# ReLU²-attention and SwiGLU feed-forward on one core: Q and K transposed by DMA, feed-forward in column halves, weights staged as float32

## The chip, the cores and the metric

The kernel runs on one core of a Trainium2 chip. The metric is the device time of one execution in microseconds (us), lower is better. The kernel before takes 549.85 us (median of 2 runs, 547.66 to 552.03). On three chips, the same kernel took 547.41, 548.23 and 549.57 us (median of 7 runs each), so differences of 1% between calls mean little; kernels of one call share a chip.

## The reference

```python
# attention: q, k, v are (8 batches, 12 heads, 448 rows, 64)
scores = scale * q @ k.T
attn   = maximum(scores, 0) ** 2 / S
x      = attn @ v              # reordered to (3584 tokens, 768)
# feed-forward: w_gate, w_val (768, 1536), w_out (1536, 768), all float32
xn  = x / sqrt(mean(x*x) + 1e-6) * rms_g
out = (silu(xn @ w_gate) * (xn @ w_val)) @ w_out
```

## The kernel before

The kernel works in bfloat16 and interleaves two streams on the engines: the feed-forward of batch b is the main stream, and attention of batch b+1, with its norm, is spread between the main stream's units. Program order fixes the order on each engine; only semaphores join the engines. PE is the matmul engine, DVE, ACT and Pool are the vector, scalar and general engines, SP issues DMAs, and SBUF is the memory on the chip. These are the parts that matter here (cuts marked with `...`).

```python
ldpool = tile_pool(name="ld", bufs=2)                 # q, k, v of a batch, two of each
...
def load_w(which, s):                                 # weights: a DMA from Pool's queue casts to bf16
    nc.gpsimd.dma_start(out=dst[:, :, s*FS:(s+1)*FS], in_=...)
...
def reorder(b, j):                                    # on DVE, for each pair of heads
    for nm in ("q", "k"):
        nc.vector.tensor_copy(out=t..., in_=ld[nm, b][:, 2*j:2*j+2, :]...)
def transposes(b, j):                                 # on PE, 8 of them, then copied by DVE
    ...
    nc.tensor.transpose(out=psT[...], in_=ldp[nm, b, j][:, c, :, :], identity=ident[:])
    nc.vector.tensor_copy(out=t[:], in_=psT[:])
def scores(b, j, cs):  ...                            # K x Q, ReLU (3 of 4 on ACT), square on DVE
def attend(b, j):      ...                            # A*V: 8 matmuls, each 64 columns of the array wide
def project(w_sb, b, fb, nm):                         # feed-forward: 6 matmuls, 128 columns wide
    for kt in range(KT):
        nc.tensor.matmul(out=ps[:], lhsT=w_sb[:, kt, fb*P:(fb+1)*P], rhs=xns[b][:, kt, :], ...)
...
for b in range(B):
    side = attention(b + 1) + [(1.1, lambda b=b: norm(b + 1))]
    alloc_ld(b + 2)
    for nm in ("q", "k", "v"):
        load(nm, b + 2)                               # Pool's queue, casting DMA
    for fn in merge(ffn(b), side, 0.0, 0.1):          # side units end 10% before the main stream
        fn()
```

Of the kernel before, what the change touches and what calls it, by code (L numbers as in the profile page):

```python
# [9 lines left out]
I32 = mybir.dt.int32  # L10
# [4 lines left out]
NCH = 4  # L15
# [3 lines left out]

# [17 lines left out]
def kernel(  # L37
# [22 lines left out]
    NT = 2 * S // P  # L60

# [4 lines left out]
    ldpool = ctx.enter_context(tc.tile_pool(name="ld", bufs=2))  # L66
    tpool = ctx.enter_context(tc.tile_pool(name="tsb", bufs=2))
    apool = ctx.enter_context(tc.tile_pool(name="attn", bufs=10))
    xpool = ctx.enter_context(tc.tile_pool(name="xT", bufs=2))
    npool = ctx.enter_context(tc.tile_pool(name="norm", bufs=2))  # L70
    hpool = ctx.enter_context(tc.tile_pool(name="hT", bufs=2))
# [4 lines left out]
    ps_m = ctx.enter_context(tc.tile_pool(name="ps_m", bufs=3, space=bass.MemoryType.PSUM))  # L76

# [6 lines left out]
    def alloc_ld(b):  # L84
        for nm in ("q", "k", "v"):
            ld[nm, b] = ldpool.tile([PC, H, NCH * D], BF16, name=nm + "b", tag=nm + "b")

    def load(nm, b, h0=0, h1=H):
        src = {"q": q, "k": k, "v": v}[nm]
        nc.gpsimd.dma_start(out=ld[nm, b][:, h0:h1, :], in_=head_rows(src, b, h0, h1))  # L90
# [4 lines left out]
    NSL = 4  # L95
    FS = F // NSL

    def load_w(which, s):
        dst, src = {"g": (wg_sb, moe_w_gate), "v": (wv_sb, moe_w_val)}[which]
        nc.gpsimd.dma_start(  # L100
            out=dst[:, :, s * FS : (s + 1) * FS],
            in_=src.rearrange("(kt p) f -> p kt f", p=P)[:, :, s * FS : (s + 1) * FS],
        )

    def load_wo(s, n):
        w = FT // n
        nc.gpsimd.dma_start(
            out=wo_sb[:, s * w : (s + 1) * w, :],
            in_=moe_w_out.rearrange("(fk p) m -> p fk m", p=P)[:, s * w : (s + 1) * w, :],
        )  # L110

    alloc_ld(0)
    load("q", 0, 0, 2)
    load("k", 0, 0, 2)
    ident = const.tile([PC, PC], BF16, name="ident", tag="ident")
    masks.make_identity(nc, ident[:])
    ones_bf = const.tile([P, P], BF16, name="ones_bf", tag="ones_bf")
    nc.vector.memset(ones_bf[:], 1.0)
    eps_col = const.tile([P, 1], FP32, name="eps_col", tag="eps_col")
    nc.vector.memset(eps_col[:], eps)  # L120
    g_sb = wpool.tile([P, KT], FP32, name="g_sb", tag="rmsg")
    nc.sync.dma_start(out=g_sb[:], in_=moe_rms_g.rearrange("(kt p) -> p kt", p=P))
    load("q", 0, 2, 6)
    load("k", 0, 2, 6)
    load("v", 0, 0, 6)
    load("q", 0, 6, 12)
    load("k", 0, 6, 12)
    load("v", 0, 6, 12)
    for s in range(NSL):
        load_w("g", s)  # L130
        load_w("v", s)
        if s == 1:
            alloc_ld(1)
            load("q", 1)
            load("k", 1)
    load("v", 1)
    load_wo(0, 2)
    load_wo(1, 2)


    xTs = {}
    qkT = {}
    ldp = {}

    def reorder(b, j):
        for nm in ("q", "k"):
            t = tpool.tile([PC, NCH, 2, D], BF16, name=nm + "p", tag=nm + "p")
            nc.vector.tensor_copy(  # L148
                out=t[:].rearrange("p c h d -> p h c d"),
                in_=ld[nm, b][:, 2 * j : 2 * j + 2, :].rearrange("p h (c d) -> p h c d", c=NCH),  # L150
            )
            ldp[nm, b, j] = t

    def transposes(b, j):
        if j == 0:
            xTs[b] = xpool.tile([P, KT, S], BF16, name="xT", tag="xT")
            reorder(b, 0)
        if j + 1 < HP:
            reorder(b, j + 1)
        psT = ps_a.tile([P, 2, S], BF16, name="psT", tag="ps_a")  # L160
        for ti, nm in enumerate(("q", "k")):
            for c in range(NCH):
                nc.tensor.transpose(  # L163
                    out=psT[:, ti, c * PC : (c + 1) * PC],
                    in_=ldp[nm, b, j][:, c, :, :],
                    identity=ident[:],
                )
        t = tpool.tile([P, 2, S], BF16, name="qkT", tag="qkT")
        nc.vector.tensor_copy(out=t[:], in_=psT[:])  # L169
        qkT[b, j] = t  # L170

    rsq = {}
    state = {"n": 0}

    def scores(b, j, cs):
        t = qkT[b, j]
        pss = []
        for c in cs:
            psS = ps_s.tile([PC, 2, 512], FP32, name="psS", tag="psS")
            for hh in range(2):  # L180
                prt = slice(hh * D, (hh + 1) * D)
                nc.tensor.matmul(  # L182
                    out=psS[:, hh, :S],
                    lhsT=t[prt, 1, c * PC : (c + 1) * PC],
                    rhs=t[prt, 0, :],
                    start=True,
                    stop=True,
                )
            pss.append(psS)
        for c, psS in zip(cs, pss):  # L190
            r = apool.tile([PC, 2, S], BF16, name="r", tag="r")
            on_dve = state["n"] % 4 == 3
            state["n"] += 1
            if on_dve:
                nc.vector.tensor_relu(out=r[:], in_=psS[:, :, :S])  # L195
            else:
                nc.scalar.activation(out=r[:], in_=psS[:, :, :S], func=ACT.Relu)  # L197
            nc.vector.tensor_tensor(out=r[:], in0=r[:], in1=r[:], op=ALU.mult)  # L198
            rsq[b, j, c] = r

    x2s = {}

    def attend(b, j):
        psAV = ps_a.tile([P, S], FP32, name="psAV", tag="ps_a")
        for c in range(NCH):
            for hh in range(2):
# [6 lines left out]
                )  # L213
        xT = xTs[b]
        nc.scalar.mul(out=xT[:, j, :], in_=psAV[:], mul=inv_attn)  # L215
        if j == 0:
# [141 lines left out]
```

## Time and profile before

| | before |
|---|---|
| time, us | 549.85 |
| span of the profiled run, us | 544.9 |
| PE / DVE / ACT busy | 89% / 62% / 46% |
| reciprocal of the norm, batch 0, 1, 7, at us | 43.95, 108.41, 491.14 |
| so one batch takes (491.14 - 108.41) / 6, us | 63.8 |

One reciprocal on DVE belongs to the norm of each batch, so the times between reciprocals give the period of a batch.

From the page of the kernel before: the span, the busy time of PE (share of the span, x instructions), and the chain of waits that ended last, by engine.

```profile
span 544.9 us, 7394 instructions
PE 485.1 (89%) x3024; PEld 236.1 (43%) x3024; DVE 338.6 (62%) x586; ACT 252.3 (46%) x369; POOL 34.4 (6%) x45
...
PE 73%; DVE 14%; ACT 8%; issue 2%; DMA 1%; POOL 0%; ACTq 0%; POOLq 0%
```

PE is the bound, and the chain runs over PE for 73% of the span.

The timeline of PE around the boundary between two batches (start us, length us, engine, line, operation, output and inputs, count; in brackets the idle time before it and who ended it):

```profile
236.43 1.48 PE L238 MATMUL psSS<-x_1924,ones_bf 128*128 128x448 bf16 x6
237.75 5.37 PE L286 MATMUL psO<-wo_sb,hT 128*128 128x256 bf16 x36
245.97 0.37 PE L163 MATMUL psT<-ident,qp 112*128 112x112 bf16 x4 [2.85 <-DVE qp L148]
246.18 0.36 PE L163 MATMUL psT<-ident,kp 112*128 112x112 bf16 x4
246.38 1.30 PE L260 MATMUL psG<-xn,wg_sb 128*128 128x448 bf16 x6
247.52 1.30 PE L260 MATMUL psV<-xn,wv_sb 128*128 128x448 bf16 x6
```

The output projection of one batch ends, PE idles 2.85 us for the reordered Q (which stands on DVE behind the norm), then come the transposes and the first gate. A group of six feed-forward matmuls starts every 1.14 us (246.38 to 247.52).

### The profile page before, as it was taken

How to read it: one execution, taken by the hardware profiler on the slowest of the kernel's cores; microseconds unless marked ns; L12 is line 12 of the kernel's file. 1: busy time of each engine (PE TensorE's matmuls, PEld its weight loads, DVE VectorE, ACT ScalarE, POOL GpSimd, SP SyncE). 2: the span in 40 equal slices, each digit the busy share in tenths (PEclk: the TensorE clock that was granted, in tenths of full speed). 3: DMA queues.
4: the chain of work that ended last, by engine and by line, in shares of the span. 5: the costliest groups of instructions: out<-in, count | busy, mean ns of one | idle time of the engine just before them, and what ended most of it. 6: DMA issues, size and time to landing. Idle time of an engine off the chain costs nothing.

```text
span 544.9 us, 7394 instructions
## 1 busy us (share of the span) xinstructions
PE 485.1 (89%) x3024; PEld 236.1 (43%) x3024; DVE 338.6 (62%) x586; ACT 252.3 (46%) x369; POOL 34.4 (6%) x45
## 2 busy tenths in 40 slices
PE   3774999879999799888999799987999899989996
PEld 1331444434444344444444444444445444444553
DVE  3886677467764677566774677656775677745210
ACT  2553454524545354535444454454545445553221
POOL 7330001000010001000010000100000000000000
PEclk9976999979999899999999999999999999999999
DMA  9999938150073402560054500733001200002013
GB/s 114 201 201 205 203 53 102 35 103 1 1 102 73 95 1 24 79 123 16 1 75 86 108 1 1 103 58 80 1 1 29 78 10 2 1 29 59 0 30 88
DMA packets 45858, 35.08 MB, mean 64 GB/s; under 512 B 2304, under 2 KB 42240, under 8 KB 45824
## 3 DMA queue, kind: packets, MB, share of 16 engines
q0 software_dynamic: 40560, 23.60, 31.7%
q1 hardware_dynamic: 5264, 11.02, 6.8%
q8 instruction: 23, 0.38, 0.3%
q14 instruction: 11, 0.09, 0.1%
HBM read 47.19 MB, written 11.01 MB: 107 GB/s over the span
## 4 chain that ended last, share of the span: by engine, by line
PE 73%; DVE 14%; ACT 8%; issue 2%; DMA 1%; POOL 0%; ACTq 0%; POOLq 0%
PE psV L260 20%; PE psG L260 20%; PE psO L286 14%; PE psAV L207 8%; PE psS L182 8%; DVE xn L249 5%; DVE rstd L246 4%; ACT r L197 4%; PE psT L163 3%; ACT L243 2%; DVE r L198 2%; DVE r L195 1%; ACT rstd L243 1%; DMA kb<-in_k_dram 1%; ACT xT L215 1%
## 5 line engine op out<-in xcount | busy, mean ns | idle before, releaser
L198 DVE TENSOR_TENSOR r<-r 112x896 bf16<-112x896 bf16 x192 | 119.3, 625 | 93.8 <-ACT r L197 91.9
L197 ACT ACTIVATE r<-psS 112x896 bf16<-112x896 f32 x144 | 127.0, 916 | 52.5 <-PE psS L182 52.4
L260 PE MATMUL psG<-xn,wg_sb 128*128 128x448 bf16 x576 | 129.4, 360 | 1.1 <-DVE xn L249 1.0
L260 PE MATMUL psV<-xn,wv_sb 128*128 128x448 bf16 x576 | 128.0, 359 | 0.0
L286 PE MATMUL psO<-wo_sb,hT 128*128 128x512 bf16 (+1 forms) x672 | 115.2, 326 | 0.0
L271 ACT ACTIVATE sil<-psG 128x448 bf16<-128x448 f32 x96 | 52.3, 545 | 102.2 <-PE psG L260 90.8
L277 DVE TENSOR_TENSOR hT<-sil,psV 128x448 bf16<-128x448 bf16 x96 | 59.4, 618 | 45.9 <-PE psV L260 37.8
L286 PEld LDWEIGHTS <-hT 128*128 128x128 bf16 x672 | 63.6, 98 | 49.2 <-issue 9.3
L182 PE MATMUL psS<-qkT 64*112 64x448 bf16 x384 | 64.5, 394 | 19.3 <-ACT r L197 7.4
L260 PEld LDWEIGHTS <-wg_sb 128*128 128x128 bf16 x576 | 53.0, 99 | 59.8 <-issue 19.2
L260 PEld LDWEIGHTS <-wv_sb 128*128 128x128 bf16 x576 | 52.3, 99 | 57.5 <-issue 19.2
L293 ACT COPY ost<-psO 128x512 f32<-128x512 f32 (+1 forms) x56 | 26.9, 480 | 81.4 <-PE psO L286 81.4
L195 DVE TENSOR_SCALAR r<-psS 112x896 bf16<-112x896 f32 x48 | 52.0, 1084 | 0.0
L207 PE MATMUL psAV<-r,vb 112*64 112x448 bf16 x384 | 47.7, 370 | 4.6 <-DVE qkT L169 3.8
L182 PEld LDWEIGHTS <-qkT 64*112 64x112 bf16 x384 | 21.1, 131 | 60.5 <-issue 55.2
L163 PE MATMUL psT<-ident,qp 112*128 112x112 bf16 x192 | 19.0, 226 | 29.6 <-DVE qp L148 29.6
L215 ACT ACTIVATE xT<-psAV 128x448 bf16<-128x448 f32 x48 | 26.1, 545 | 33.7 <-PE psAV L207 33.7
L163 PEld LDWEIGHTS <-qp 112*128 112x128 bf16 x192 | 14.0, 103 | 40.9 <-DVE qp L148 31.9
L207 PEld LDWEIGHTS <-vb 112*64 112x64 bf16 x384 | 19.1, 111 | 28.9 <-issue 21.4
L246 DVE RECIPROCAL rstd<-rstd 128x448 f32<-128x448 f32 x8 | 23.6, 2953 | 12.8 <-ACT rstd L243 12.8
L169 DVE COPY qkT<-psT 128x896 bf16<-128x896 bf16 x48 | 29.8, 620 | 2.3 <-PE psT L163 2.1
L249 DVE SCALAR_TENSOR_TENSOR xn<-xT,g_sb,rstd 128x448 bf16<-128x448 bf16 x48 | 29.3, 680 | 0.3
(39 smaller groups left out, 157.6 us busy)
## 6 DMA issues: line engine op xcount, KB each, us to landing
qb<-in_q_dram POOLq DMA_DIRECT2D x7, 672.0 KB, 7.3
kb<-in_k_dram POOLq DMA_DIRECT2D x7, 672.0 KB, 9.8
vb<-in_v_dram POOLq DMA_DIRECT2D x7, 672.0 KB, 8.1
out_dram<-ost SPq DMA_DIRECT2D x8, 336.0 KB, 2.8
wg_sb<-in_moe_w_gate_dram POOLq DMA_DIRECT2D x4, 576.0 KB, 20.2
wv_sb<-in_moe_w_val_dram POOLq DMA_DIRECT2D x4, 576.0 KB, 21.8
wo_sb<-in_moe_w_out_dram POOLq DMA_DIRECT2D x2, 1152.0 KB, 28.3
out_dram<-ost SPq DMA_DIRECT2D x8, 288.0 KB, 5.3
```

The costliest lines, as they stand in the source:

```text
L163: nc.tensor.transpose(out=psT[:, ti, c * PC : (c + 1) * PC], in_=ldp[nm, b, j][:, c, :, :], identity=ident[:],)
L182: nc.tensor.matmul(out=psS[:, hh, :S], lhsT=t[prt, 1, c * PC : (c + 1) * PC], rhs=t[prt, 0, :], start=True, stop=True,)
L195: nc.vector.tensor_relu(out=r[:], in_=psS[:, :, :S])
L197: nc.scalar.activation(out=r[:], in_=psS[:, :, :S], func=ACT.Relu)
L198: nc.vector.tensor_tensor(out=r[:], in0=r[:], in1=r[:], op=ALU.mult)
L207: nc.tensor.matmul(out=psAV[hh * D : (hh + 1) * D, :], lhsT=ld["v", b][:, 2 * j + hh, c * D : (c + 1) * D], rhs=rsq[b, j, c][:, hh, :], st ...
L246: nc.vector.reciprocal(out=rstd[:], in_=rstd[:])
L249: nc.vector.scalar_tensor_tensor(out=xn[:, kt, :], in0=xTs[b][:, kt, :], scalar=g_sb[:, kt : kt + 1], in1=rstd[:], op0=ALU.mult, op1=ALU.mult,
L260: nc.tensor.matmul(out=ps[:], lhsT=w_sb[:, kt, fb * P : (fb + 1) * P], rhs=xns[b][:, kt, :], start=(kt == 0), stop=(kt == KT - 1),)
L271: nc.scalar.activation(out=s[:], in_=psG[:], func=ACT.Silu)
L277: nc.vector.tensor_tensor(out=hTs[b // 2][:, fb, o : o + S], in0=sil[b, fb][:], in1=psV[:], op=ALU.mult)
L286: nc.tensor.matmul(out=ps[:, :w], lhsT=hTs[i][:, fk, t * P : (t + 1) * P], rhs=wo_sb[:, fk, o : o + w], start=(fk == 0), stop=(fk == FT - 1),)
```

## The change

It has four parts.

1. Q and K of batches 2 to 7 are reordered by two large DVE copies and transposed by two DMA transposes issued by SP. Batches 0 and 1 keep transposes on PE, now without reorder.
2. All feed-forward matmuls, and the sum of squares, are issued as two halves of 64 columns, the tiling that A*V already had.
3. The weights come as float32 by SP's DMA queue into a pool of 7 staging buffers, and Pool casts them.
4. To make room, `q` and `k` have one buffer instead of two, and so have the pools of the attention output and of the norm. DVE takes one ReLU in six instead of one in four. Attention of batch 1 is spread over the last 70% of the first feed-forward, to its very end.

```diff
-    ldpool = ctx.enter_context(tc.tile_pool(name="ld", bufs=2))
+    ldpool = ctx.enter_context(tc.tile_pool(name="ld", bufs=1))          # v keeps bufs=2
 ...
+    def fetch_w(which, s):                       # SP, float32 into the staging pool
+        ...
+        return nc.sync.dma_start(out=st[:], in_=src)
+    def cast_w(which, s, eng):                   # eng is nc.gpsimd
+        eng.tensor_copy(out=dst, in_=st[:])
 ...
+    def reorder(b):
+        t = late["reord"].tile([PC, 2, NCH, H, D], BF16, name="kqp", tag="kqp")
+        for ti, nm in enumerate(("k", "q")):
+            nc.vector.tensor_copy(out=t[:, ti]..., in_=ld[nm, b][:]...)
+    def dma_transposes(b):
+        t = tpool.tile([P, 2, NCH, HP, PC], BF16, name="kqT", tag="kqT", bufs=1)
+        for ti in range(2):
+            nc.sync.dma_start_transpose(out=t[:, ti]..., in_=src[:, ti]...)
 ...
+    def halves(ps, w, lhsT, rhs, start, stop):
+        for hf in range(2):
+            prt = slice(hf * HALF, (hf + 1) * HALF)
+            nc.tensor.matmul(out=ps[prt, :w], lhsT=lhsT[:, prt], rhs=rhs, start=start, stop=stop)
 ...
-            side = attention(b + 1) + [(1.1, lambda b=b: norm(b + 1))]
+            side = attention(b + 1, False)
+            def prepare(b=b):
+                if b + 2 < B:
+                    reorder(b + 2)
+                    dma_transposes(b + 2)
+            side += [(0.0, prepare), (1.1, lambda b=b: norm(b + 1))]
         if b + 2 < B:
             alloc_ld(b + 2)
             for nm in ("q", "k", "v"):
                 load(nm, b + 2)
```

More of the change, by code (lines that the diff above doesn't have):

```diff
@@ L9 @@
 FP32 = mybir.dt.float32
-I32 = mybir.dt.int32
 BF16 = mybir.dt.bfloat16
@@ L60 @@
     NT = 2 * S // P
+    HALF = P // 2
     ctx.enter_context(tc.manual_schedule())
@@ L65 @@
     wpool = ctx.enter_context(tc.tile_pool(name="weights", bufs=1))
-    ldpool = ctx.enter_context(tc.tile_pool(name="ld", bufs=2))
+    ldpool = ctx.enter_context(tc.tile_pool(name="ld", bufs=1))
     tpool = ctx.enter_context(tc.tile_pool(name="tsb", bufs=2))
     apool = ctx.enter_context(tc.tile_pool(name="attn", bufs=10))
-    xpool = ctx.enter_context(tc.tile_pool(name="xT", bufs=2))
-    npool = ctx.enter_context(tc.tile_pool(name="norm", bufs=2))
-    hpool = ctx.enter_context(tc.tile_pool(name="hT", bufs=2))
+    xpool = ctx.enter_context(tc.tile_pool(name="xT", bufs=1))
+    npool = ctx.enter_context(tc.tile_pool(name="norm", bufs=1))
+    hpool = ctx.enter_context(tc.tile_pool(name="hT", bufs=1))
     spool = ctx.enter_context(tc.tile_pool(name="sig", bufs=3))
@@ L76 @@
     ps_m = ctx.enter_context(tc.tile_pool(name="ps_m", bufs=3, space=bass.MemoryType.PSUM))
+    late = {}
     def head_rows(t, b, h0, h1):
@@ L84, in alloc_ld @@
     def alloc_ld(b):
-        for nm in ("q", "k", "v"):
+        for nm in ("q", "k"):
             ld[nm, b] = ldpool.tile([PC, H, NCH * D], BF16, name=nm + "b", tag=nm + "b")
+        ld["v", b] = ldpool.tile([PC, H, NCH * D], BF16, name="vb", tag="vb", bufs=2)
     def load(nm, b, h0=0, h1=H):
         src = {"q": q, "k": k, "v": v}[nm]
-        nc.gpsimd.dma_start(out=ld[nm, b][:, h0:h1, :], in_=head_rows(src, b, h0, h1))
+        return nc.gpsimd.dma_start(out=ld[nm, b][:, h0:h1, :], in_=head_rows(src, b, h0, h1))
     wg_sb = wpool.tile([P, KT, F], BF16, name="wg_sb", tag="wg")
@@ L94 @@
     wo_sb = wpool.tile([P, FT, DM], BF16, name="wo_sb", tag="wo")
-    NSL = 4
+    NSL = 6
     FS = F // NSL
-    def load_w(which, s):
-        dst, src = {"g": (wg_sb, moe_w_gate), "v": (wv_sb, moe_w_val)}[which]
-        nc.gpsimd.dma_start(
-            out=dst[:, :, s * FS : (s + 1) * FS],
-            in_=src.rearrange("(kt p) f -> p kt f", p=P)[:, :, s * FS : (s + 1) * FS],
-        )
-    def load_wo(s, n):
-        w = FT // n
-        nc.gpsimd.dma_start(
-            out=wo_sb[:, s * w : (s + 1) * w, :],
-            in_=moe_w_out.rearrange("(fk p) m -> p fk m", p=P)[:, s * w : (s + 1) * w, :],
-        )
@@ L112 @@
-    alloc_ld(0)
-    load("q", 0, 0, 2)
-    load("k", 0, 0, 2)
-    ident = const.tile([PC, PC], BF16, name="ident", tag="ident")
-    masks.make_identity(nc, ident[:])
-    ones_bf = const.tile([P, P], BF16, name="ones_bf", tag="ones_bf")
-    nc.vector.memset(ones_bf[:], 1.0)
-    eps_col = const.tile([P, 1], FP32, name="eps_col", tag="eps_col")
-    nc.vector.memset(eps_col[:], eps)
-    g_sb = wpool.tile([P, KT], FP32, name="g_sb", tag="rmsg")
-    nc.sync.dma_start(out=g_sb[:], in_=moe_rms_g.rearrange("(kt p) -> p kt", p=P))
@@ L123 @@
-    load("q", 0, 2, 6)
-    load("k", 0, 2, 6)
-    load("v", 0, 0, 6)
-    load("q", 0, 6, 12)
-    load("k", 0, 6, 12)
-    load("v", 0, 6, 12)
-    for s in range(NSL):
-        load_w("g", s)
-        load_w("v", s)
-        if s == 1:
-            alloc_ld(1)
-            load("q", 1)
-            load("k", 1)
-    load("v", 1)
-    load_wo(0, 2)
-    load_wo(1, 2)
+    stage = {}
+    def fetch_w(which, s):
+        if which == "o":
+            st = late["stage"].tile([P, 2, DM], FP32, name="wst", tag="wst")
+            src = moe_w_out.rearrange("(fk p) m -> p fk m", p=P)[:, 2 * s : 2 * s + 2, :]
+        else:
+            st = late["stage"].tile([P, KT, FS], FP32, name="wst", tag="wst")
+            w = {"g": moe_w_gate, "v": moe_w_val}[which]
+            src = w.rearrange("(kt p) f -> p kt f", p=P)[:, :, s * FS : (s + 1) * FS]
+        stage[which, s] = st
+        return nc.sync.dma_start(out=st[:], in_=src)
@@ L141 @@
+    def cast_w(which, s, eng):
+        st = stage.pop((which, s))
+        if which == "o":
+            dst = wo_sb[:, 2 * s : 2 * s + 2, :]
+        else:
+            dst = {"g": wg_sb, "v": wv_sb}[which][:, :, s * FS : (s + 1) * FS]
+        if eng is nc.scalar:
+            eng.copy(out=dst, in_=st[:])
+        else:
+            eng.tensor_copy(out=dst, in_=st[:])
     xTs = {}
     qkT = {}
-    ldp = {}
-    def reorder(b, j):
-        for nm in ("q", "k"):
-            t = tpool.tile([PC, NCH, 2, D], BF16, name=nm + "p", tag=nm + "p")
-            nc.vector.tensor_copy(
-                out=t[:].rearrange("p c h d -> p h c d"),
-                in_=ld[nm, b][:, 2 * j : 2 * j + 2, :].rearrange("p h (c d) -> p h c d", c=NCH),
-            )
-            ldp[nm, b, j] = t
@@ L154, in transposes @@
-    def transposes(b, j):
-        if j == 0:
-            xTs[b] = xpool.tile([P, KT, S], BF16, name="xT", tag="xT")
-            reorder(b, 0)
-        if j + 1 < HP:
-            reorder(b, j + 1)
-        psT = ps_a.tile([P, 2, S], BF16, name="psT", tag="ps_a")
-        for ti, nm in enumerate(("q", "k")):
-            for c in range(NCH):
-                nc.tensor.transpose(
-                    out=psT[:, ti, c * PC : (c + 1) * PC],
-                    in_=ldp[nm, b, j][:, c, :, :],
-                    identity=ident[:],
-                )
+    kqT = {}
@@ new lines, with pe_transposes @@
+    rsq = {}
+    x2s = {}
+    state = {"n": 0}
+    def pe_transposes(b, j):
+        psT = ps_m.tile([P, 2, S], BF16, name="psT", tag="mm")
+        for ti, nm in enumerate(("k", "q")):
+            for c in range(NCH):
+                for hh in range(2):
+                    nc.tensor.transpose(
+                        out=psT[hh * D : (hh + 1) * D, ti, c * PC : (c + 1) * PC],
+                        in_=ld[nm, b][:, 2 * j + hh, c * D : (c + 1) * D],
+                        identity=ident[:],
+                    )
@@ L170, in transposes @@
         qkT[b, j] = t
-    rsq = {}
-    state = {"n": 0}
+    def reorder(b):
+        t = late["reord"].tile([PC, 2, NCH, H, D], BF16, name="kqp", tag="kqp")
+        for ti, nm in enumerate(("k", "q")):
+            nc.vector.tensor_copy(
+                out=t[:, ti].rearrange("p c h d -> p h c d"),
+                in_=ld[nm, b][:].rearrange("p h (c d) -> p h c d", c=NCH),
+            )
+        late["kqp", b] = t
+    def dma_transposes(b):
+        t = tpool.tile([P, 2, NCH, HP, PC], BF16, name="kqT", tag="kqT", bufs=1)
+        src = late["kqp", b]
+        for ti in range(2):
+            nc.sync.dma_start_transpose(
+                out=t[:, ti].rearrange("p c j s -> p (c j) s"),
+                in_=src[:, ti].rearrange("p c h d -> p (c h d)"),
+            )
+        kqT[b] = t
     def scores(b, j, cs):
-        t = qkT[b, j]
         pss = []
         for c in cs:
-            psS = ps_s.tile([PC, 2, 512], FP32, name="psS", tag="psS")
+            psS = ps_s.tile([P, 2, 512], FP32, name="psS", tag="psS")
             for hh in range(2):
                 prt = slice(hh * D, (hh + 1) * D)
-                nc.tensor.matmul(
-                    out=psS[:, hh, :S],
-                    lhsT=t[prt, 1, c * PC : (c + 1) * PC],
-                    rhs=t[prt, 0, :],
-                    start=True,
-                    stop=True,
+                if b in kqT:
+                    t = kqT[b]
+                    flat = t[prt].rearrange("p t c j s -> p (t c j s)")
+                    o = (c * HP + j) * PC
+                    lhsT, rhs, m = flat[:, o : o + P], t[prt, 1, :, j, :], P
+                else:
+                    t = qkT[b, j]
+                    flat = t[prt].rearrange("p t s -> p (t s)")
+                    lhsT, rhs, m = flat[:, c * PC : c * PC + P], t[prt, 1, :], P
+                nc.tensor.matmul(
+                    out=psS[:m, hh, :S], lhsT=lhsT, rhs=rhs, start=True, stop=True
                 )
@@ L191, in scores @@
             r = apool.tile([PC, 2, S], BF16, name="r", tag="r")
-            on_dve = state["n"] % 4 == 3
+            on_dve = state["n"] % 6 == 5
             state["n"] += 1
             if on_dve:
-                nc.vector.tensor_relu(out=r[:], in_=psS[:, :, :S])
+                nc.vector.tensor_relu(out=r[:], in_=psS[:PC, :, :S])
             else:
-                nc.scalar.activation(out=r[:], in_=psS[:, :, :S], func=ACT.Relu)
+                nc.scalar.activation(out=r[:], in_=psS[:PC, :, :S], func=ACT.Relu)
             nc.vector.tensor_tensor(out=r[:], in0=r[:], in1=r[:], op=ALU.mult)
             rsq[b, j, c] = r
-    x2s = {}
     def attend(b, j):
@@ L213, in attend, with attention @@
                 )
+        if j == 0:
+            xTs[b] = xpool.tile([P, KT, S], BF16, name="xT", tag="xT")
+            x2s[b] = npool.tile([P, KT, S], BF16, name="x2", tag="x2")
         xT = xTs[b]
         nc.scalar.mul(out=xT[:, j, :], in_=psAV[:], mul=inv_attn)
-        if j == 0:
-            x2s[b] = npool.tile([P, KT, S], BF16, name="x2", tag="x2")
         nc.vector.tensor_tensor(out=x2s[b][:, j, :], in0=xT[:, j, :], in1=xT[:, j, :], op=ALU.mult)
-    def attention(b):
-        units = [(0.4, lambda: transposes(b, 0))]
+    def attention(b, by_pe):
+        units = []
+        if by_pe:
+            units.append((0.4, lambda: pe_transposes(b, 0)))
         for j in range(HP):
             units.append((0.5, lambda j=j: scores(b, j, (0, 1))))
-            if j + 1 < HP:
-                units.append((0.4, lambda j=j: transposes(b, j + 1)))
+            if by_pe and j + 1 < HP:
+                units.append((0.4, lambda j=j: pe_transposes(b, j + 1)))
             units.append((0.5, lambda j=j: scores(b, j, (2, 3))))
@@ L237, in norm @@
         for kt in range(KT):
-            nc.tensor.matmul(
-                out=psSS[:], lhsT=ones_bf[:], rhs=x2s[b][:, kt, :],
-                start=(kt == 0), stop=(kt == KT - 1),
-            )
-        rstd = npool.tile([P, S], FP32, name="rstd", tag="rstd", bufs=1)
+            halves(psSS, S, ones_bf, x2s[b][:, kt, :], kt == 0, kt == KT - 1)
+        rstd = npool.tile([P, S], FP32, name="rstd", tag="rstd")
         nc.scalar.activation(
@@ L253, in norm @@
         xns[b] = xn
+        i = b // 2
         if b % 2 == 0:
-            hTs[b // 2] = hpool.tile([P, FT, 2 * S], BF16, name="hT", tag="hT")
+            pool = hpool if i % 2 == 0 else late["hpool"]
+            hTs[i] = pool.tile([P, FT, 2 * S], BF16, name="hT", tag="hT")
     def project(w_sb, b, fb, nm):
@@ L259, in project @@
         for kt in range(KT):
-            nc.tensor.matmul(
-                out=ps[:], lhsT=w_sb[:, kt, fb * P : (fb + 1) * P], rhs=xns[b][:, kt, :],
-                start=(kt == 0), stop=(kt == KT - 1),
-            )
+            halves(ps, S, w_sb[:, kt, fb * P : (fb + 1) * P], xns[b][:, kt, :], kt == 0, kt == KT - 1)
         return ps
@@ L285, in outproj @@
         for fk in range(FT):
-            nc.tensor.matmul(
-                out=ps[:, :w], lhsT=hTs[i][:, fk, t * P : (t + 1) * P], rhs=wo_sb[:, fk, o : o + w],
-                start=(fk == 0), stop=(fk == FT - 1),
+            halves(
+                ps, w, hTs[i][:, fk, t * P : (t + 1) * P], wo_sb[:, fk, o : o + w],
+                fk == 0, fk == FT - 1,
             )
@@ L314, in ffn @@
         return units
-    for fn in merge([], attention(0) + [(1.1, lambda: norm(0))]):
-        fn()
-    for b in range(B):
+    alloc_ld(0)
+    load("q", 0, 0, 2)
+    load("k", 0, 0, 2)
+    ident = const.tile([PC, PC], BF16, name="ident", tag="ident")
+    masks.make_identity(nc, ident[:])
+    ones_bf = const.tile([P, P], BF16, name="ones_bf", tag="ones_bf")
+    nc.vector.memset(ones_bf[:], 1.0)
+    eps_col = const.tile([P, 1], FP32, name="eps_col", tag="eps_col")
+    nc.vector.memset(eps_col[:], eps)
@@ new lines, with feed, both, ahead @@
+    g_sb = wpool.tile([P, KT], FP32, name="g_sb", tag="rmsg")
+    nc.sync.dma_start(out=g_sb[:], in_=moe_rms_g.rearrange("(kt p) -> p kt", p=P))
+    load("q", 0, 2, 6)
+    load("k", 0, 2, 6)
+    load("v", 0, 0, 6)
+    load("q", 0, 6, 12)
+    last_k = load("k", 0, 6, 12)
+    last_v = load("v", 0, 6, 12)
+    with tc.tile_pool(name="stage", bufs=7) as sp:
+        late["stage"] = sp
+        order = []
+        for s in range(NSL):
+            order += [("g", s), ("v", s)]
+        order += [("o", s) for s in range(FT // 2)]
+        first = fetch_w(*order[0])
+        tc.add_manual_dep(
+            first.ins if hasattr(first, "ins") else first,
+            (last_k.ins if hasattr(last_k, "ins") else last_k).name,
+            mybir.DependencyInfo(mybir.DependencyClass.Sync, mybir.DependencyReason.DATA),
+            reason="weights after the first batch",
+        )
+        for w in order[1:7]:
+            fetch_w(*w)
+        for fn in merge([], attention(0, True) + [(1.1, lambda: norm(0))]):
+            fn()
+        def feed(n):
+            cast_w(*order[n], nc.gpsimd)
+            if n + 7 < len(order):
+                fetch_w(*order[n + 7])
+        units = ffn(0)
+        fed = 0
+        for _ in range(4):
+            feed(fed)
+            fed += 1
+        alloc_ld(1)
+        side = attention(1, True) + [(1.1, lambda: norm(1))]
+        main = []
+        for n, (c, f) in enumerate(units):
+            def both(n=n, f=f):
+                state["u"] = n
+                f()
+            main.append((c, both))
+        done = {"fed": fed}
+        def ahead(n):
+            while done["fed"] < min(n, len(order)):
+                feed(done["fed"])
+                done["fed"] += 1
+        seq = []
+        for n, (c, f) in enumerate(units):
+            def step(n=n, f=f):
+                if n < 2 * FT:
+                    ahead(n // 2 + 5)
+                if n == 6:
+                    for nm in ("q", "k", "v"):
+                        load(nm, 1)
+                if n == 2 * FT - 6:
+                    ahead(len(order))
+                f()
+            seq.append((c, step))
+        for fn in merge(seq, side, 0.3, 0.0):
+            fn()
@@ L319 @@
+    late["reord"] = ctx.enter_context(tc.tile_pool(name="reord", bufs=1))
+    late["hpool"] = ctx.enter_context(tc.tile_pool(name="hT1", bufs=1))
+    alloc_ld(2)
+    for nm in ("q", "k", "v"):
+        load(nm, 2)
+    reorder(2)
+    dma_transposes(2)
+    for b in range(1, B):
         side = []
         if b + 1 < B:
-            side = attention(b + 1) + [(1.1, lambda b=b: norm(b + 1))]
+            side = attention(b + 1, False)
[4 more added lines that the diff above has]
+            side += [(0.0, prepare), (1.1, lambda b=b: norm(b + 1))]
```

## The prediction

> What bounds the kernel now. The page shows PE busy 89% of a 544.9 us span, DVE 62%, ACT 46%; the chain that ended last is 73% PE. By the timeline six 448-column feed-forward matmuls start every 1.135 us, 189 ns each, and the last batch alone runs without a gap: the feed-forward is at PE's rate, so halving its matmuls cannot speed them. The reciprocals of the norms give the period of a batch: 108.4 to 491.1 us for six, 63.8 us each. PE work at the pace seen is about 52 us. The rest, per batch:
> - A*V interludes: 8 matmuls at 94.5 ns are 0.76 us but take 0.99. 0.23 us x6 = 1.4 us. The Trainium skill (TensorEngine Tiling, Key Properties) says that changing the tiling mode drains the engine; this gap agrees. Score interludes lose the same, x12 = 2.7 us.
> - score stalls on ReLU where score units stand together: about 2.3 us.
> - the boundary: PE idles 2.86 us for the reordered Q (waits view: 17.1 us in six), then runs its first two groups in 2.24 and 1.73 us instead of 1.135 (cold clock): about 4.5 us.
>
> What the change does.
> 1. DMA transposes: off PE go six transpose units of 0.40 us (2.4 us a batch), off DVE six 0.62 us copies. The reorder stays on DVE in two pieces (estimate 2 x 1.7 us from 293 ns per 512 elements).
> 2. Feed-forward in 64-column halves, as A*V: A*V drains vanish, -1.4 us a batch. A*V pairs already run two halves at once, so I expect the feed-forward pace unchanged; the 256-wide output halves (54 ns for load plus matmul) may slip a little.
> 3. Fewer side units, one ReLU in six instead of four on DVE: score stalls shrink, -1.5 us.
> 4. Boundary: scores of the next batch, first in PE's order, need both DMA transposes, which start only after the reorder, about 5 us of main work before the batch ends. The Trainium skill (DMA: Bandwidth & Descriptors, Latency and other measured facts) gives 261 GB/s, 2.6 us for each 688 KB; no trace here shows it, and I estimate 3 to 5 us each, in turn. Then the boundary costs about as before.
> Sum: about -5.5 us for each of six periods, -33 us.
>
> Startup. Attention of batch 0 is DVE-bound (17.5 of 20 us busy in 20 to 40 us); reorders (0.59 per head pair) and some ReLUs leave it, -6 us, but Pool casts (18[...]) may hold up DVE and give most of it back. Weights should still be ahead of the first feed-forward; it gains 5 us. But at its end norm 1 comes at 97%, and the reorder of batch 2 stands on DVE behind that norm, then two DMA transposes, with PE waiting: about 20 us idle where before lost 5. Net +5 us.
>
> Predicted: 549.85 - 33 + 5, about 521 us; 8 in 10 for 497 to 546. Chances: faster 0.76, same 0.16, slower 0.08.
>
> What would show it: no PE transposes after batch 1; feed-forward pairs still 189 ns; reciprocals 57 to 59 us apart from batch 2; one PE gap of 15 to 20 us near 100 to 120 us waiting on the transposes; shorter score waits; DVE waiting during Pool casts before 80 us.
>
> What would make it wrong: DMA transposes of 8 us or more put a wait at each boundary and eat the gain; halves that don't overlap fully lengthen all of the feed-forward; Pool casts above 4 us starve the first feed-forward.

## The result, and the profile after

The changed kernel takes 602.47 us (2 runs, 601.91 and 603.04), the kernel before 549.85 us: slower, ratio 1.0972 with a 95% interval of 1.0849 to 1.1095. Ratios here are the mean time of one kernel's runs over that of the other's of the same rounds, so not quite the ratio of the medians quoted. Executions over 1.5% slower than the fastest of the same kernel are left out of the means.

| | before | after |
|---|---|---|
| time, us | 549.85 | 602.47 |
| PE / DVE / ACT busy, us | 485.1 / 338.6 / 252.3 | 468.7 / 305.5 / 264.2 |
| reciprocals of batch 0 and 1, at us | 43.95, 108.41 | 45.72, 113.46 |
| from reciprocal to reciprocal, batches 1 to 7, us | 67.3, 63.4, 64.3, 61.7, 64.3, 61.7 | 83.5, 73.8, 72.7, 74.2, 72.8, 57.4 |

From the page of the changed kernel, the same lines, and the chain by line:

```profile
span 601.3 us, 10714 instructions
PE 468.7 (78%) x4704; PEld 261.6 (44%) x4704; DVE 305.5 (51%) x450; ACT 264.2 (44%) x385; POOL 54.8 (9%) x53
...
PE 66%; DMA 16%; DVE 9%; ACT 6%; issue 1%; SPq 0%; POOL 0%; DVEq 0%; ACTq 0%; POOLq 0%
PE psG L238 19%; PE psV L238 19%; DMA kqT<-kqp 16%; PE psO L238 13%; PE psS L183 7%; PE psAV L202 6%; ACT r L194 3%; DVE r L195 3%; DVE rstd L248 2%; DVE xn L251 2%; ACT L245 1%; ACT rstd L245 1%; DVE r L192 1%; DMA kb<-in_k_dram 1%; ACT ost L294 1%
```

PE has less work than before, as intended (16.4 us less busy), and yet the span grew: the chain now has 16% in the DMA transposes. The waits view of PE names it (total us, times, longest us):

```profile
PE psS L183 <- DMA kqT<-kqp: 96.1, 6, 30.0
PE psG L238 <- DVE xn L251: 7.9, 8, 4.4
PE psS L183 <- ACT r L194: 6.2, 11, 1.0
```

The wait that ends at the first scores of each batch is 96.1 us in six, 30.0 us the longest. Here is PE at a later boundary:

```profile
267.95 1.33 PE L238 MATMUL psSS<-x,ones_bf 128*64 128x448 bf16 x12
269.09 5.41 PE L238 MATMUL psO<-wo_sb,hT 128*64 128x256 bf16 x72
288.63 0.93 PE L183 MATMUL psS<-kqT 64*128 64x448 bf16 x4 [14.14 <-DMA kqT<-kqp]
289.49 2.45 PE L238 MATMUL psG<-xn,wg_sb 128*64 128x448 bf16 x12
291.73 2.45 PE L238 MATMUL psV<-xn,wv_sb 128*64 128x448 bf16 x12
294.12 0.55 PE L183 MATMUL psS<-kqT 64*128 64x448 bf16 x4
294.60 1.33 PE L238 MATMUL psG<-xn,wg_sb 128*64 128x448 bf16 x12
295.76 1.30 PE L238 MATMUL psV<-xn,wv_sb 128*64 128x448 bf16 x12
```

PE idles 14.14 us, and then it also runs its first two groups at half speed (2.24 and 2.39 us from start to start) before it is back at 12 halves in 1.16 us (294.60 to 295.76), which is the pace of before. The granted clock, the share of full clock that the profile reports for PE, was 0.50 from 288.6 to 294.1 us and 1.00 in the 5.9 us after. The halves themselves cost nothing: in the last batch, which runs alone, a group of 12 starts every 1.13 us.

What did the other engines do in those 20 us? These are lines of DVE, then SP's queue, then Pool, at the same boundary:

```profile
265.17 0.95 DVE L152 COPY kqp<-kb 112x3072 bf16<-112x3072 bf16 x1
266.03 0.95 DVE L152 COPY kqp<-qb 112x3072 bf16<-112x3072 bf16 x1
...
266.94 19.18 SPq L162 DMA_TRANSPOSE kqT<-kqp  x2
...
267.28 0.93 POOL L92 DMA_DIRECT2D qb<-in_q_dram  x1 [71.03 <-DVE kqp L152]
268.21 0.93 POOL L92 DMA_DIRECT2D kb<-in_k_dram  x1
269.13 0.94 POOL L92 DMA_DIRECT2D vb<-in_v_dram  x1
```

This is the clue. The reorder reads the only buffers of Q and K. When it is done, two things become possible at once: the DMA transposes, which PE will need in some 8 us, and the loads of the next batch, which nobody needs for 50 us. Pool had waited 71.03 us for just this moment, so 2 MB of loads start 0.3 us after the transposes. The Trainium skill (DMA: Bandwidth & Descriptors, Queues, rings and completion order) says that each DMA engine takes turns between the queues that have work, a packet at a time, and the same page (Issuing engines are not separate DMA queues) that transfers issued by different engines run on the same 16 DMA engines. The DMA view of this stretch, 267 to 289 us, agrees: first how busy the 16 DMA engines were, in tenths, in 40 slices of 0.55 us (9 is 90% or more), then the queues. q0 holds Pool's loads, q1 the transposes and output stores (packets, MB, and the time that the packets took as a share of 16 engines' time).

```profile
DMA  9712979999999999999999999999999999999999
...
q0 software_dynamic: 4080, 2.06, 70.8%
q1 hardware_dynamic: 5737, 2.11, 51.1%
```

From the seventh slice on the engines were busy at 90% or more, and the loads' packets took the larger part of the time (70.8 against 51.1; these are sums of packet times, which together exceed 100% here). The last boundary is a control that the kernel itself provides. Batch 7 is the last, nothing is left to load, and PE there waited only 2.85 us for its transposes; that period is 57.4 us, where I had predicted 57 to 59.

### The profile page after: what moved, and what is told of

It is laid out like the page before. It is cut to its first block, busy times and chain, and to the rows that moved or that the text cites. A ratio compares the mean times of both kernels' runs of the same rounds, so it can differ in the third digit from the quotient of the medians.

```text
span 601.3 us, 10714 instructions
## 1 busy us (share of the span) xinstructions
PE 468.7 (78%) x4704; PEld 261.6 (44%) x4704; DVE 305.5 (51%) x450; ACT 264.2 (44%) x385; POOL 54.8 (9%) x53
## 4 chain that ended last, share of the span: by engine, by line
PE 66%; DMA 16%; DVE 9%; ACT 6%; issue 1%; SPq 0%; POOL 0%; DVEq 0%; ACTq 0%; POOLq 0%
PE psG L238 19%; PE psV L238 19%; DMA kqT<-kqp 16%; PE psO L238 13%; PE psS L183 7%; PE psAV L202 6%; ACT r L194 3%; DVE r L195 3%; DVE rstd L248 2%; DVE xn L251 2%; ACT L245 1%; ACT rstd L245 1%; DVE r L192 1%; DMA kb<-in_k_dram 1%; ACT ost L294 1%
## 5 line engine op out<-in xcount | busy, mean ns | idle before, releaser
L238 PE MATMUL psG<-xn,wg_sb 128*64 128x448 bf16 x1152 | 135.9, 369 | 8.0 <-DVE xn L251 7.9
L238 PE MATMUL psV<-xn,wv_sb 128*64 128x448 bf16 x1152 | 131.8, 365 | 0.0
L183 PE MATMUL psS<-kqT 64*128 64x448 bf16 x288 | 43.5, 369 | 99.7 <-DMA kqT<-kqp 96.1
L238 PE MATMUL psO<-wo_sb,hT 128*64 128x512 bf16 (+1 forms) x1344 | 114.9, 326 | 0.0
L238 PEld LDWEIGHTS <-wg_sb 128*64 128x64 bf16 x1152 | 66.2, 113 | 65.7 <-issue 32.6
L238 PEld LDWEIGHTS <-hT 128*64 128x64 bf16 x1344 | 77.3, 110 | 34.2 <-issue 4.5
L238 PEld LDWEIGHTS <-wv_sb 128*64 128x64 bf16 x1152 | 68.1, 114 | 47.8 <-issue 13.1
L278 DVE TENSOR_TENSOR hT<-sil,psV 128x448 bf16<-128x448 bf16 x96 | 59.4, 618 | 57.4 <-PE psV L238 52.8
L294 ACT COPY ost<-psO 128x512 f32<-128x512 f32 (+1 forms) x56 | 26.9, 480 | 72.7 <-PE psO L238 72.7
L214 DVE TENSOR_TENSOR x<-xT 128x448 bf16<-128x448 bf16 x48 | 19.2, 399 | 32.1 <-ACT xT L213 32.1
L192 DVE TENSOR_SCALAR r<-psS 112x896 bf16<-112x896 f32 x32 | 34.6, 1083 | 0.0
L183 PE MATMUL psS<-qkT 64*128 64x448 bf16 x96 | 18.6, 437 | 9.2 <-ACT r L194 5.4
## 6 DMA issues: line engine op xcount, KB each, us to landing
wst<-in_moe_w_gate_dram SPq DMA_DIRECT2D x6, 768.0 KB, 10.4
```

The costliest lines, as they stand in the source:

```text
L183: nc.tensor.matmul(out=psS[:m, hh, :S], lhsT=lhsT, rhs=rhs, start=True, stop=True)
L192: nc.vector.tensor_relu(out=r[:], in_=psS[:PC, :, :S])
L238: nc.tensor.matmul(out=ps[prt, :w], lhsT=lhsT[:, prt], rhs=rhs, start=start, stop=stop)
L278: nc.vector.tensor_tensor(out=hTs[b // 2][:, fb, o : o + S], in0=sil[b, fb][:], in1=psV[:], op=ALU.mult)
L294: nc.scalar.copy(out=ost[:, o : o + w], in_=ps[:, :w])
```

## The experiments

Theory A: the transposes are slow only because they share the DMA engines with the loads that the same reorder sets free. Rival B: transposes of this size are slow by themselves, or stand behind the output stores in SP's queue. Further questions were whether the column halves and the weight staging cost or save anything, and what the first boundary, with its wait of 30 us, is made of.

### The loads held back

```diff
             for nm in ("q", "k", "v"):
-                load(nm, b + 2)
+                ins = load(nm, b + 2)
+                add_manual_dep(ins, <last DMA transpose issued>, Sync, DATA)
```

The dependence is a wait on the transposes' completion, in Pool's queue, where nothing else stands behind it but loads.

> The changed kernel, but the loads of Q, K, V of a later batch (3 to 7) wait until the transposes of the batch before them have landed. Theory A (the transposes share the 16 DMA engines with those loads, which the reorder itself sets free): two transposes take about 10 us instead of 14 to 22, PE's wait at a boundary falls from 14 to 18 us to about 3 us as at the one boundary with no loads (2.85 us), the first from 30 to about 20; time about 602 - 10 - 52 = 540 us. Rival B (a DMA transpose of this size is slow by itself, or stands behind output stores in SP's queue): waits stay above 12 us, time above 590 us.

Measured: 530.16 us against 547.41 for the kernel before (4 and 7 runs), ratio 0.9674 (0.9606 to 0.9742), correct. The same boundary in its profile, SP's queue, Pool and PE:

```profile
238.02 6.73 SPq L162 DMA_TRANSPOSE kqT<-kqp  x2
...
247.14 0.93 POOL L92 DMA_DIRECT2D qb<-in_q_dram  x1 [54.06 <-DVE xn L251]
...
246.60 0.56 PE L183 MATMUL psS<-kqT 64*128 64x448 bf16 x4 [2.36 <-DMA kqT<-kqp]
247.09 1.33 PE L238 MATMUL psG<-xn,wg_sb 128*64 128x448 bf16 x12
```

From the first issue to PE's start are now 8.6 us (238.02 to 246.60) where it was 21.7 (266.94 to 288.63), the wait fell from 14.14 to 2.36 us, and the first gate runs at full speed. The six waits sum to 30.3 us instead of 96.1, of which 17.5 are the first. (The brackets put Pool's wait down to DVE; by the edit it waits for the completion of the transposes, and Pool starts 0.5 us after PE does.) Theory A holds, with 10 us more gain than I had expected. Part of it is the clock: after the long wait it was 0.50 for 5.5 us, here after the short one 1.00 (246.6 to 252 us; not so at every boundary, for after 2.27 us of waiting at 362.09 the scores were slow too), and the mean over the span rose from 0.901 to 0.948. Rival B falls: nothing about the transposes or SP's order was changed. The later periods, 56.9 to 59.9 us, are now close to the 57 to 59 that I had predicted.

Of the 17.5 us left at the first boundary, 8.8 pass before the transposes are issued (PE is free at 111.92, they start at 120.72), because the reorder of batch 2 stands on DVE behind norm 1; the other 8.7 are the transposes. That loads in flight slow the transposes is shown by this run. That the two meet in the queues of the DMA engines, and not elsewhere on their way, rests on the page and the full engines in the DMA view.

### Only K and V held back

The same edit for `nm in ("k", "v")`. It asks for a dose: one load of three collides.

> The same, but only K and V are held back; Q still collides. Theory A makes the wait a matter of the bytes in flight beside the transposes: one load of 5.2 us of packets (a third of 15.5) instead of three, so waits of about 8 us at a boundary and 25 us at the first, time about 566 us, between the changed kernel and the one that holds all three. Rival B: no different from the changed kernel, 600 us. Rival C (any load at all, whatever its size, stops the transposes): as the changed kernel.

Measured: 559.85 us (median of the three fast runs, 559.8 to 561.12); ratio to before 1.0216 (1.0153 to 1.0278). It lies between 530 and 602, near the 566 expected. The profile of this kernel fell into a fourth run of 1616 us, in which PE alone was busy for 1569 us; no other run of any kernel showed that, I have no explanation for it, and I use nothing of it.

> The kernel that holds K and V only, once more for its profile (the first profile fell in a run three times as long). Theory A: waits of 7 to 9 us at the boundaries and about 22 us at the first; two transposes in 10 to 12 us; time 560 us.

Measured: 562.12 us (one run, so its state is unknown, and on another chip, but it agrees with the three fast ones). The waits view and two boundaries of it:

```profile
PE psS L183 <- DMA kqT<-kqp: 55.5, 6, 21.5
...
199.51 0.93 PE L183 MATMUL psS<-kqT 64*128 64x448 bf16 x4 [8.12 <-DMA kqT<-kqp]
331.29 0.93 PE L183 MATMUL psS<-kqT 64*128 64x448 bf16 x4 [10.41 <-DMA kqT<-kqp]
```

The next four boundaries wait 6.0 to 10.4 us, the last, with nothing left to load, 2.8. With no load, one and three colliding, the waits of all six boundaries are 30.3, 55.5 and 96.1 us. The delay goes with the bytes in flight, which speaks against rival C (that any load, whatever its size, stops the transposes).

### All transposes on PE

```diff
-            side = attention(b + 1, False)
+            side = attention(b + 1, True)
-            side += [(0.0, prepare), (1.1, lambda b=b: norm(b + 1))]
+            side += [(1.1, lambda b=b: norm(b + 1))]
```

> The changed kernel with the transposes of all batches on PE, column halves and weight staging kept. No wait on transposes by DMA. PE gets 6 transpose units of 0.40 us a batch back. If all of the loss sits in the DMA transposes, a batch takes about 60 us (57.4, the last undisturbed period, plus 2.4) and the whole about 538 us, faster than before by 2%. If column halves or staging cost something that the waits hide, it is not faster than before (550 us).

Measured: 528.15 us, ratio 0.9632 (0.9583 to 0.9682), correct. Without any DMA transpose the changed kernel beats the one before by 3.7%. It is on a par with the kernel that holds the loads (530.16), so at this point the DMA transposes, even without collisions, were worth nothing in total: what they take off PE they give back in the 17.5 us at the first boundary and 2 to 3 us at the others. The reciprocals show it: from the third on, a batch takes 58.3 us with them and 59.6 without, but the period before that takes 70.4 against 62.5. The expected 538 us was too high as a sum only: the batches take 60.0 us as expected, and 112.4 us to the second reciprocal, six batches and 53.6 us after the last make 526.

### Feed-forward 128 columns wide again, loads held

```diff
-        for hf in range(2):
-            prt = slice(hf * HALF, (hf + 1) * HALF)
-            nc.tensor.matmul(out=ps[prt, :w], lhsT=lhsT[:, prt], rhs=rhs, start=start, stop=stop)
+        nc.tensor.matmul(out=ps[:, :w], lhsT=lhsT[:, :], rhs=rhs, start=start, stop=stop)
```

> As the one that holds all three loads, but feed-forward matmuls 128 columns wide again. Theory (column halves save the drain around A*V, about 0.23 us at each of 6 interludes a batch): slower than that one by about 10 us in all, the A*V interlude 0.99 us instead of 0.76. Rival (the halves cost PE something, or do nothing): same or faster.

Measured: 535.34 us against 530.16 with halves, on the same chip (4 runs each, 533.68 to 537.62 and 528.69 to 532.94). PE at one A*V interlude, first with 128 columns:

```profile
258.91 1.31 PE L236 MATMUL psG<-xn,wg_sb 128*128 128x448 bf16 x6
260.14 0.95 PE L202 MATMUL psAV<-r,vb 112*64 112x448 bf16 x8
261.02 1.31 PE L236 MATMUL psV<-xn,wv_sb 128*128 128x448 bf16 x6
```

then with halves (the kernel that holds the loads):

```profile
315.55 1.30 PE L238 MATMUL psG<-xn,wg_sb 128*64 128x448 bf16 x12
316.69 0.93 PE L202 MATMUL psAV<-r,vb 112*64 112x448 bf16 x8
317.45 1.30 PE L238 MATMUL psV<-xn,wv_sb 128*64 128x448 bf16 x12
```

A gate group with the A*V behind it takes 2.11 us with the switch and 1.90 without, so 0.21 us is saved each time. This agrees with what the Trainium skill (TensorEngine Tiling (Array Packing), Key Properties) says of a change of tiling mode, that it drains the engine. Six interludes in seven batches would be 9 us; the whole kernel gained 5. The rest was given back: with halves PE reaches the boundary earlier, and its wait for the transposes is longer (30.3 us in six against 26.8).

### Weights by casting DMA again, transposes on PE

The staging, its fetches and casts are replaced by the `load_w` of the kernel before, in the kernel with all transposes on PE.

> The kernel with all transposes on PE (528 us), with the weights fetched by casting DMAs on Pool's queue as in the kernel before, in place of the float32 staging by SP and the casts on Pool. Theory: Pool's casts read SBUF beside DVE's two-input products and lengthen them in the start (products 0.62 us alone, up to 1.9 us beside a cast; in all about 8 us of products and 2 us of xn), and DVE bounds that stretch. Without casts the first reciprocal comes at 37 to 40 us instead of 44.6 and the whole is about 520 us. Rival (staging pays, weights come sooner): 528 us or more, and PE waits for weights.

Measured: 521.4 us, ratio 0.9511 (0.9446 to 0.9576), on another chip than the 528.15. The first reciprocal comes at 40.71 us instead of 44.61, the second at 105.42 instead of 112.37, and after it the periods are the same within 0.4 us. DVE in the first attention, with Pool's casts beside it (transposes on PE, staging kept):

```profile
28.28 1.88 DVE L195 TENSOR_TENSOR r<-r 112x896 bf16<-112x896 bf16 x1
...
47.60 5.88 DVE L251 SCALAR_TENSOR_TENSOR xn<-xT,g_sb,rstd 128x448 bf16<-128x448 bf16 x6
```

and without casts:

```profile
32.62 0.62 DVE L182 TENSOR_TENSOR r<-r 112x896 bf16<-112x896 bf16 x1 [0.47 <-ACT r L181]
...
43.70 3.67 DVE L238 SCALAR_TENSOR_TENSOR xn<-xT,g_sb,rstd 128x448 bf16<-128x448 bf16 x6
```

The same product took up to 1.88 us beside a cast, and without casts all 192 of them took 0.61 to 0.63 us; the six xn took 5.88 against 3.67. The Trainium skill (SBUF — State Buffer, Who interferes with whom) says that a DVE instruction with two SBUF inputs contends with a GpSimd instruction that reads SBUF; this agrees. The staging as a whole cost about 7 us. That the casts are all of it was not separated: the edit also changes when the weights arrive.

### Batch 2 prepared inside the first feed-forward, loads held

```diff
-        side = attention(1, True) + [(1.1, lambda: norm(1))]
+        side = side[:18] + [load k, q, v of batch 2] + side[18:] + [reorder(2), dma_transposes(2), norm(1)]
-        for fn in merge(seq, side, 0.3, 0.0):
+        for fn in merge(seq, side, 0.1, 0.1):
```

> The kernel that holds the loads (530 us), with batch 2 loaded, reordered and transposed inside the first feed-forward ahead of norm 1, and attention of batch 1 spread with 0.1 head and 0.1 tail (staging pool of 5 buffers, to make room). If the 17.5 us wait at the first boundary is only the late load and reorder of batch 2, it falls to below 5 us: about 515 us. If the weights or batch 1's own loads are what comes late there, little changes.

Measured: 529.52 us, and the result was WRONG (relative error 0.34). The mistake is mine (the edit also takes the staging pool from 7 buffers to 5, to make room): with a head of 0.1 the first transposes of batch 1 come before its load in program order, so they read a buffer that had not been filled. Its times still tell something about the waits. The wait on the transposes at the first boundary fell from 17.5 to 4.3 us, as expected, but PE waited 13.2 us for batch 1's own K instead. The last sentence of the expectation was the one that came true: the wait had only moved.

### Transposes early in the feed-forward, loads not held

```diff
-        t = tpool.tile([...], BF16, name="kqT", tag="kqT", bufs=1)
+        t = late["kqT"].tile([...], BF16, name="kqT", tag="kqT")          # a pool with bufs=2
-            side += [(0.0, prepare), (1.1, lambda b=b: norm(b + 1))]
+            side = side[:6] + [(0.0, prepare)] + side[6:] + [(1.1, lambda b=b: norm(b + 1))]
```

> The changed kernel with two buffers for the transposed Q and K and the reorder and transposes after a third of the feed-forward's side work; the loads are not held and still collide. Theory: the collision costs only because it falls on the boundary; the pair takes its 14 to 22 us under 35 us of PE work, waits at the boundaries 0, only the first one of 30 us stays: 533 to 538 us. Rival (collisions slow the kernel in some other way): waits gone but time above 550 us.

Measured: 535.68 us, ratio 0.9769 (0.9713 to 0.9825), correct. The waits view has one wait on the transposes left, the first:

```profile
PE psS L183 <- DMA kqT<-kqp: 29.7, 1, 29.7
```

SP's queue shows that each later pair still takes 12 to 13 us where the loads of Q and K run beside it (1.38 MB; that of V now comes later) and 7.4 where none does; nobody waits for it. So the collision costs only where it falls on PE's next need.

### Transposes early, and loads held

> As the one before, with the loads held as well. Against the kernel that holds the loads alone (530 us) the five waits of about 2.5 us go: 517 to 521 us, with the first wait of 17.5 us still there. If the boundary is bound by the norm's chain on DVE anyway, no gain: 528 to 530 us.

Measured: 523.13 us, 2 us above the range, ratio 0.954 (0.9486 to 0.9594), correct. The edit is the two above together. The first wait is 17.6 us and no other is left; the difference of 12.5 us to the kernel before this one is the first boundary (29.7 against 17.6). Against holding alone (on another chip) it gained 7 us of the 12.8 us of waits that it removed: PE now waits for the norm's xn at the boundaries (11.4 us in all, against 7.9). Both answers in the expectation were partly right.

### All together

Column halves; weights by casting DMA, which leaves room for two buffers of Q and K; batches 1 and 2 loaded early; the reorder and transposes right after the last scores of the batch before, and those of batch 2 inside the first feed-forward, after 16 of its 24 side units; loads held; attention of batch 1 spread from the first unit on, ending 10% before the end.

```diff
-    ldpool = ctx.enter_context(tc.tile_pool(name="ld", bufs=1))
+    ldpool = ctx.enter_context(tc.tile_pool(name="ld", bufs=2))
 ...
-            side += [(0.0, prepare), (1.1, lambda b=b: norm(b + 1))]
+            side = side[:16] + [(0.0, prepare)] + side[16:] + [(1.1, lambda b=b: norm(b + 1))]
```

> Everything that the runs point to: column halves, weights by casting DMA (no staging), two buffers for Q and K so that batches 1 and 2 are loaded early, reorder and DMA transposes of the next but one batch right after the last scores of the batch before (batch 2 inside the first feed-forward), loads held until the transposes have landed, attention of batch 1 spread from the first unit on. Expected: first reciprocal near 41 us, second near 102, then 57 us a batch, no wait on the transposes above 3 us: 498 to 505 us. If early loads of batches 1 and 2 delay the weights, the second reciprocal comes later and the time is 510 us or more.

Measured: 493.48 us (4 runs, 493.3 to 493.72), the kernel before 549.57 on the same chip; ratio 0.8985 (0.8942 to 0.9028), correct. It beats both kernels, and it lies 4.5 us below the range that I expected; the two reciprocals came some 2 us earlier than expected, and the period is 0.7 us shorter. The boundary in its profile:

```profile
211.04 5.40 PE L227 MATMUL psO<-wo_sb,hT 128*64 128x256 bf16 x72
216.38 0.55 PE L172 MATMUL psS<-kqT 64*128 64x448 bf16 x4
216.86 0.80 PE L227 MATMUL psG<-xn,wg_sb 128*64 128x448 bf16 x6
217.87 0.38 PE L227 MATMUL psG<-xn,wg_sb 128*64 128x448 bf16 x2 [0.21 <-DVE xn L240]
```

PE goes from the output projection straight into the next scores and waits only some 0.2 us at a time for the norm here (9.4 us in the whole run, the longest 4.1). The period is 56.3 us ((437.74 - 99.67) / 6), the second reciprocal comes at 99.67 us, and PE is busy 93% of the span.

### The same with transposes on PE

> The kernel before this one in the call with all transposes on PE instead of DMA. What the DMA transposes are worth when nothing collides: six units of 0.40 us a batch on PE, 2.4 us for each of six batches, so 12 to 17 us slower than that one (512 to 518 us). If PE had that time free anyway, the same.

Measured: 514.43 us on the same chip, ratio to before 0.9361 (0.9308 to 0.9415), correct: in the range expected, but 21 us slower than with DMA transposes where I had expected 12 to 17. The period is 59.8 us against 56.3. Of these 3.4 us, six transpose units of 0.40 us account for 2.4. The rest I did not separate; score waits on ACT's ReLU are 12.2 us in this profile against 7.9. The edit also drops DVE's reorder and the hold on the loads, which has nothing to wait for. So the DMA transposes are worth 4% once nothing collides.

## Why the prediction was wrong

I predicted 521 us, faster with a chance of 0.76; measured were 602. Point by point:

- **"PE bound, feed-forward pace unchanged by the halves": right.** 12 halves start every 1.13 to 1.16 us.
- **"Score stalls shrink, -1.5 us" a batch: about half.** PE's waits for a ReLU are 14.8 us in the whole profile before, 9.2 with the loads held, so 0.8 us in each of seven batches.
- **"A*V drains vanish": right in kind.** 0.21 us per interlude against 0.23 predicted; in the total 5 us instead of 8 to 9, because part went into a longer wait.
- **"DMA transposes ... I estimate 3 to 5 us each, in turn": right for transposes alone.** A pair took 8.6 us from issue to use in the run without collision, against 6 to 10 for two in turn.
- **"Then the boundary costs about as before": the step that failed.** PE's wait was taken to stay as before (2.86 us); instead PE waited 14.1 to 17.6 us at four boundaries and 30.0 at the first. I costed the transposes with the DMA engines to themselves, although I knew that the change gives Q and K a single buffer. I did not ask what else the reorder sets free at that instant. It frees 2 MB of loads, which in the kernel before went out in the middle of a batch, at 83 us for instance, when nothing on PE depended on a DMA. Holding them took 72 us off the time (602.47 to 530.16, on two chips), which is nearly the whole distance from the prediction (81 us).
- **"Net +5 us" for the start: mis-sized as well, for two reasons.** I expected about 20 us idle at the first boundary; it was 30.0, and 17.5 without the collision, so this is the same error. And the weight staging gave back more than the 6 us that DVE was to gain: the first reciprocal came at 45.72 us, not before 43.95, and staging cost 7 us in the experiment. Holding the loads gives 530 us; an estimate that takes off the 7 us of the staging comes to 523, near the predicted 521. No run had these two together and nothing else.
- **What I listed as the danger, "DMA transposes of 8 us or more put a wait at each boundary", was the right symptom.** But I tied it to the transposes' own speed and gave slower a chance of 0.08.

## What to carry to other kernels

When a change takes away a buffer, ask which instruction now releases the next transfer, and what else starts at that instant; here loads that nobody needed for 50 us stretched a transfer that was needed in 8 us from 8.6 to 21.7. Where an urgent transfer shares the DMA engines with a bulk one, either make the bulk one wait for it or issue the urgent one early enough to be slow. Before a saving is added up, follow it to the next wait: here the halves, the removed transposes and the early loads each gave part of theirs back there.

## What the Trainium skill lacked or had wrong

- DMA: Bandwidth & Descriptors, Latency and other measured facts, gives a DMA transpose 261 GB/s, measured on one kernel with a non-contiguous middle dimension, and more for a contiguous one. Neither was reached here: from 239 to 244 us of the run with the loads held, with nothing but the two transposes (688 KB each, SBUF to SBUF) in flight, the DMA view shows 192 GB/s on average.
- No page says what a DMA transpose costs beside other traffic. Here the pair took 21.7 us with three loads (2.06 MB written) beside it and 8.6 us with none, and the waits over six boundaries grew 30.3, 55.5, 96.1 us with none, one and three loads.
- TensorEngine Tiling (Array Packing), Key Properties, says that a mode change drains the engine, without a cost. Here going into and out of A*V cost 0.21 us more than staying in one mode.
- SBUF — State Buffer, Who interferes with whom, says who blocks whom, without a duration for a product with two SBUF inputs beside a cast. Here casts of 128x1536 float32 elements on Pool (1.5 to 1.9 us each) lengthened a DVE product of 112x896 from 0.62 to as much as 1.88 us.
